# Moving four squares, filling products and three expert layers in the hand-made order of a fused attention and mixture kernel

## The chip, the cores and the metric

One core of a Trainium2 chip runs the whole program. The metric is the device time of one launch in microseconds, the median of several runs. The engines are named as in the profile: PE (TensorE), DVE (VectorE), ACT (ScalarE), POOL (GpSimd), and SP (SyncE), which here issues every DMA.

## The reference

Three stages follow one another. Attention with a block mask over 64 heads, 576 rows of 64; a soft mixture of eight experts over the 4608 resulting rows of 512; then a gated product with three matrices.

```python
scores = np.where(mask, scale * q @ k.T, -1e9)          # mask: blocks of 64
x = softmax(scores) @ v                                  # -> 4608 x 512
logits = x @ phi                                         # 32 slots
slot_input = softmax(logits, 0).T @ x                    # 32 x 512
for e in range(8):                                       # 4 slots each
    slot_out[e] = np.maximum(slot_input[e] @ w1[e], 0) @ w2[e]
x = softmax(logits, 1) @ slot_out
out = ((x @ w1_) * (x @ w2_)) @ w3 @ w_out
```

As only 32 slots exist, the last line is computed by way of products of pairs of slots: w3 and w_out are multiplied once (1024 x 512), and pairs of slots are weighted with it.

## The kernel before, in words

The core handles the 64 heads as 32 pairs, four pairs to a batch. `Plan` holds one entry for every operation: its engine, an estimated duration, what it comes after, and a due time from the tables `OFF`, `EARLY`, `LATE`, `TAIL` and `POST`. `order()` plays this plan through with its own estimates and writes out one list, and each engine executes its part of the list strictly in that order. "After" entries shape only this list; on the chip an instruction waits for the data and buffers that it truly uses. PE has two queues in the plan, `row` (sorted by due time) and `fill` (the products `W`); a `W` is taken whenever it fits ahead of the next row entry.

Names that the change touches, in order of time:

- `M0`-`M3`, `mT`, `Q0`-`Q3`: coarse scores for row maxima, the turning of these maxima, and the exact scores of a pair. `warm` issues products of zeros on PE ahead of such an operation. `run` does so where the plan saw PE idle for over 0.5 us ahead of an `M`, a `Q` or an `mT` of pairs 0 and 1: before `M2` of pair 0 (4 products of 256 columns), `M3` of pair 1 (1), `M1` of pair 1 (2) and `mT` of pair 0 (6).
- `E0`-`E3` (ACT, line 607): exponentials of the scores. `V0`, `V1` (PE, line 632): their products with v, copied out by `c0`, `c1` (ACT, line 641). `lgT` (PE, line 706) turns a batch's logits; `LTe` (ACT, lines 771 to 776) is its exponential.
- `bl`, `bm`, `b1` to `b4`: the background. 28 times, SP loads 512 KB of a 64-bit weight (`bl`, line 1026); ACT squares its high halves (`bm`, line 1039), DVE does three bit operations (`b1` to `b3`), and `b4` combines both. `bm` and `b1` wait for the load.
- `wl` 0 to 15 (SP, line 1058): 2 MB of expert weights each, first layers even, second layers odd, into five windows used in turn; `wl` i waits for the layer that used its window. `rl` (SP, line 1084): twelve pieces of w3 of 512 KB into buffers freed by products `W`, squared by `nq` (ACT, line 1097), rebuilt by `n1` to `n4` (DVE), split by `ph` (ACT) and `pl` (POOL, both by helper lines 1045 and 1047).
- `W` (PE, line 1134): 192 products of w3 with w_out. Piece i is the twelve products 12i to 12i+11. The list takes pieces 0, 2, 4, 6, then 1, 3, 5, 7, then 8 to 15. Three products are kept for the last stage, and five more wait for the last second layer.
- `L1`, `L2` (PE, lines 1155 and 1176): first and second layer of expert e. Between them lie `hs`, `hT`, `re` (ACT, PE, ACT). In the list before, `L1` 2 stands behind `W` 12, `L1` 3 behind `W` 22, and `L1` 4 behind `W` 60.
- `so`, `sS`, `sd`, then four times `ab`, `ac`, `aT`, `aa`, `ad`: the slots' outputs are multiplied with w1_ and w2_ in four sums `ab` (PE, line 1200), copied (`ac`), turned (`aT`, PE, line 1211) and taken apart by ACT (`aa`) and DVE (`ad`, both line 1216). The list has `ab` 0, `aT` 0, `ab` 1, `aT` 1 and so on. `G` 0 on DVE is the first product of slot pairs, and `ad` 1 stands behind it. All four turns write one PSUM bank.
- Then, outside the plan, the sums over pairs (PE, line 1296) and the output's products (line 1359).

Of the kernel before, what the change touches and what calls it, by code (L numbers as in the profile page):

```python
# [27 lines left out]
SP = 640  # L28
# [3 lines left out]
def warm(nc, keep, ps, n, w=128):  # L32

    for _ in range(n):
        nc.tensor.matmul(ps[:, 0:w], lhsT=keep["zeros"][:, 0:128], rhs=keep["zeros"][:, 0:w], start=True, stop=True)
# [5 lines left out]
           M2=(-125.6823, -227.9619, -295.6467, -206.3959), M3=(-194.0205, -267.9342, -226.9977, -208.1606),  # L41
# [9 lines left out]
           M2=(-2844.3708, -1088.7161, -992.9072, -317.549), M3=(-2623.525, -1855.0865, -787.0927, -742.624),  # L51
# [31 lines left out]
WAIT = dict(PE=0.0, DVE=10616.85007, ACT=6722.41331, POOL=7334.5673, SP=12439.66901)  # L83
PERIOD, HELD, SLIP, WIN0, WIN1 = 100.0, 8, 0.1, 20, 29
BG0, BGS = 3.0, 1.0
BESIDE = {8: 0, 9: 2, 26: 4, 27: 6}
LATE_W3 = [i for i in range(16) if i not in BESIDE.values()]
PLACE = (0, 4, 1, 5, 2, 6, 3, 7)
# [11 lines left out]
class Plan:  # L100
# [136 lines left out]
    def experts(self, N):  # L237
        B = N // NP_B - 1
        quarter = lambda x: [f"{x}{i}" for i in range(4)]
        scores = lambda *ns: [(q, n) for n in ns for q in quarter("Q")]  # L240
        pair = lambda n: [(x, n) for x in ("V0", "V1", "SU", "P0", "P1", "P3")]
        at = lambda n, x: [(x, n)] if n >= 0 else []
        op = lambda name, n, *a, **k: self.op((name, n), *a, **k)
        free = {i: pair(N - 2 + PLACE[i] // 3) for i in range(8) if PLACE[i] < 6}
        free[5] = [("ts", 1), ("lt", 2), ("LTe", B - 1), ("lgT", B - 1)]
        free[7] = [("lt", 3), ("la", 3), ("cTd", B - 1)]
        out = {0: [("sub", N - 2)], 1: [("sub", N - 1)], 2: [("V0", N - 3), ("V1", N - 3), ("cT", B - 1)], 3: [("pl", 0), ("pl", 2)],
               **{c: [("mI", 0), ("ws", 0)] for c in range(4, 8)}}
        win = {0: [("Q0", 6)], 1: scores(N - 4, N - 3), 2: scores(N - 2, N - 1), 3: scores(N - 1) + [(f"sx{i}", B - 1) for i in range(4)], 4: [("S", B - 1)] + [(x, n) for n in (N - 2, N - 1) for x in ("V0", "V1")]}
        for i in range(16):  # L250
            self.due = lambda t: (WIN0 if i == 0 else WIN1 if i < 4 else N) * PERIOD + (POST[f"wl{i}"] if i else 0.)
            op("wl", i, "SP", .4, win[i] if i in win else [(("L1", "L2")[(i - 5) % 2], (i - 5) // 2)], lat=2.5, load=4.97)
            if i < 4:
                self.due = lambda t: N * PERIOD + POST["zm"] + i
                op("zm", i, "POOL", .5, win[i] + [("pl", 6)] * (i == 0))
        self.due = lambda t: N * PERIOD + POST[t]
        for c in range(8):
            op("wh", c, "ACT", .55, [("b4", c)] + out[c], due=f"wh{c}")
            op("wo", c, "POOL", 1.26, [("wh", c)], due=f"wh{c}")
        for i in range(16):  # L260
            f, g = divmod(i, 2)
            t = self.due
            if i in LATE_W3:
                q = LATE_W3.index(i)
                prev = LATE_W3[q - 1] if q else None
                op("rl", i, "SP", .43, free[i] if i < 8 else [("W", 24 * (f - 4) + 12 * g + 11)], lat=2.5, load=1.25, due=f"rl{i}")
                op("nq", i, "ACT", .62, [("rl", i)] + [("b4", 27) if q == 0 else ("n4", prev)], due=f"nn{i}")
                op("n1", i, "DVE", .69, [("rl", i), ("n4", prev) if q else ("wr", 0)], 1, due=f"nn{i}")
                op("n2", i, "DVE", .69, [("n1", i)], due=f"nn{i}", late=.1)
                op("n3", i, "DVE", .69, [("n2", i)], due=f"nn{i}", late=.2)  # L270
                op("n4", i, "DVE", .69, [("n3", i), ("nq", i)] + [("pl", LATE_W3[q - 2]) if q > 1 else ("b3", 27)], free="n1", due=f"nn{i}", late=.3)
            op("ph", i, "ACT", .58, [("n4", i)] if i in LATE_W3 else [("b4", next(j for j in BESIDE if BESIDE[j] == i))] + free[i], due=f"ph{i}")
            op("pl", i, "POOL", 1.26, [("ph", i)], due=f"ph{i}")
        order = [(f, j) for g in (0, 12) for f in range(4) for j in range(g, g + 12)] + [(f, j) for f in range(4, 8) for j in range(24)]
        for n, (f, j) in enumerate(order[:-LATER]):
            c, i = divmod(j, 3)
            deps = [("ph", 2 * f + c // 4)] if j % 12 == 0 or f == 0 else []
            if j % 12 == 2:
                deps += [("pl", 2 * f + c // 4)]
            if n >= len(order) - HELD:  # L280
                deps += [("L2", 7)]
            if f == 0:
                deps += [("wh", c)] if i == 0 else [("wo", c)] if i == 1 else []
            op("W", 24 * f + j, "PE", .2325, deps, int(j == 0), filler=True, due="W")
        for f in range(7):
            op("We", f, "ACT", .5, [("W", 24 * f + 23), ("wo", f)], free=("W", 24 * f), due="We", late=10. * f)
            if f > 3:
                op("Wh", f, "ACT", .55, [("We", f)], due="Wh", late=10. * f)
                op("Wl", f, "POOL", 1.26, [("Wh", f)], due="Wh", late=10. * f)
        for e in range(8):  # L290
            op("L1", e, "PE", 1.75, [("wl", 2 * e), ("sC", 0)] + at(e - 1, "L2"), 1, mode="quarters", due="L", late=100. * e)
            op("hs", e, "ACT", .3, [("L1", e)] + at(e - 2, "hT"), free="L1", due="L", late=100. * e + 10)
            op("hT", e, "PE", .2, [("hs", e)], 1, due="L", late=100. * e + 20)
            op("re", e, "ACT", .22, [("hT", e), ("zm", e // 2)], free="hT", due="L", late=100. * e + 30)
            op("L2", e, "PE", 1.74, [("re", e), ("wl", 2 * e + 1)], int(e == 0), mode="quarters", due="L", late=100. * e + 40)
        op("so", 0, "ACT", .55, [("L2", 7), ("z6", 0)], free=("L2", 0), due="gh", late=-1.)
        op("sS", 0, "PE", 0.81, [("so", 0), ("hT", 6)], 1, due="end")
        op("sd", 0, "DVE", .25, [("sS", 0)], free="sS", due="end")
        for t in range(4):
            op("ab", t, "PE", .9, [("sd", 0)], 1, mode="quarters", due="end", late=.1 + .4 * t)  # L300
            op("ac", t, "ACT", .25, [("ab", t)], free=("ab", t), due="We", late=-5. - (3))
            op("aT", t, "PE", .1, [("ac", t)], int(t == 0), due="end", late=.3 + .4 * t)
            op("aa", t, "ACT", .4, [("aT", t)], due="We", late=-5. - (4))
            if t < 2:
                op("ad", t, "DVE", .3, [("aT", t)], due="end", late=.5 if t == 0 else .8 + t)
        op("g0", 0, "POOL", .4, [("L2", 7)], due="end")
        op("ow", 0, "DVE", .3, [("L2", 6)], due="end")
        for f in range(4):
            op("gh", f, "ACT", .55, [("We", f), ("L2", 5 if f < 2 else 7)], due="gh", late=10. * f)
            op("gl", f, "POOL", 1.26, [("gh", f)], due="gh", late=10. * f)  # L310
        op("G", 0, "DVE", 2.05, [("aa", 0), ("ad", 0), ("L2", 6)], due="end", late=.7)
        op("Gc", 0, "ACT", .6, [("G", 0)], due="We", late=-5.5)
# [7 lines left out]
    def order(self):  # L320
# [13 lines left out]
        while len(out) < len(ops):  # L334
# [14 lines left out]
                    if best is None or c[0] < best[0]:  # L349
                        best = c[0], e, c[1]  # L350
            t, e, k = best
            o, slot, idle = ops[k], None, t - free[e]
            del ready[e][k]
            end = t + o["dur"]
            if e == "PE":
# [19 lines left out]
            if o["free"]:  # L375
                for i in held[o["free"]]:
                    bank[i] = done[k]
            out.append((t, len(out), k, slot, idle if e == "PE" and k[1] < 2 else 0.))
            for a in then.get(k, ()):
                waits[a] -= 1  # L380
                if not waits[a]:
                    ready[ops[a]["eng"]][a] = max(done[x] for x in ops[a]["after"])
        return [o[2:] for o in sorted(out)]


class Ring:
# [11 lines left out]
class Attn:  # L398
# [581 lines left out]
        self.constants()  # L980

    def run(self):
        for (name, n), slot, idle in Plan(self.nb).order():
            if idle > .5 and (name[0] in "MQ" or name == "mT") and n < 2:
                warm(self.nc, self.keep, self.bank(slot), int(4.5 * idle - 1), 256)
            f = getattr(self, "op_" + name, None) or getattr(self.rest, "op_" + name, None)
            if f:
                f(n, slot)
            else:
                f = getattr(self, "op_" + name[:-1], None) or getattr(self.rest, "op_" + name[:-1])  # L990
                f(n, slot, int(name[-1]) if name[-1].isdigit() else name[-1])
# [555 lines left out]
```

## Time and profile before

| what | value |
|---|---|
| median of 3 runs | 563.34 us (562.89 to 563.6) |
| the profiled execution | 562.72 us, of which the span of its instructions is 560.7 us |
| PE busy | 544.9 us, 97% of the span |
| DVE, POOL, ACT busy | 394.6, 332.6, 322.2 us |
| mean granted PE clock | 0.997 of full speed |
| DMA | 116.97 MB, mean 209 GB/s |

A busy engine has an instruction in flight; it is not thereby at its peak. The idle time before an instruction is shown in brackets with what ended it. The granted clock is given as a share of 2.4 GHz; its other level is 1.2 GHz. Times from here on are microseconds from the start of the span.

### The profile page before, as it was taken

The page shows a single profiled execution, that of the slowest core. Times are in us where ns is not written, and L with a number is a line of the kernel's source. Part 1 is how long each engine was busy: PE and PEld are TensorE (multiplying, and loading weights), DVE is VectorE, ACT ScalarE, POOL GpSimd, SP SyncE. Part 2 cuts the span into 40 slices and gives each one's busy share as a digit, 9 for nine tenths or more (in the row PEclk, how much of TensorE's full clock was granted, in tenths as well). Part 3 has the DMA queues.
Part 4 walks back from the last instruction along what each step waited for, and adds up shares of the span by engine and source line. Part 5 has one row for each costly group of instructions (what it writes and reads, how often), then busy time and mean ns, then how long its engine had stood idle before and what let it go on. Part 6 is the DMA issues. An engine that isn't in the chain of part 4 may idle for free.

```text
span 560.7 us, 14190 instructions
## 1 busy us (share of the span) xinstructions
PE 544.9 (97%) x5527; PEld 407.3 (73%) x5527; DVE 394.6 (70%) x720; ACT 322.2 (57%) x636; POOL 332.6 (59%) x244
## 2 busy tenths in 40 slices
PE   8899999999999999999999989998999999999997
PEld 4777878787878787877778665455568678888885
DVE  5778877898988988988773469207579486665650
ACT  3856768577677696785857624214443355454451
POOL 5798996997978979979976526103530022313220
PEclk9999999999999999999999999989999999999999
DMA  7245685556558465565557977999822058557622
GB/s 251 97 164 178 200 308 177 173 184 210 161 181 233 143 215 191 156 209 167 155 159 259 388 274 288 425 420 427 357 65 77 1 150 263 191 177 252 207 102 110
DMA packets 39514, 116.97 MB, mean 209 GB/s; under 512 B 5532, under 2 KB 15996, under 8 KB 37384
## 3 DMA queue, kind: packets, MB, share of 16 engines
q1 hardware_dynamic: 39448, 116.08, 60.4%
q8 instruction: 43, 0.70, 0.5%
q14 instruction: 23, 0.19, 0.1%
HBM read 105.75 MB, written 10.45 MB: 207 GB/s over the span
## 4 chain that ended last, share of the span: by engine, by line
PE 81%; DMA 10%; DVE 3%; ACT 2%; POOL 1%; issue 1%; SPq 0%; DVEq 0%; ACTq 0%; POOLq 0%
PE ps L1359 16%; PE ps L584 16%; PE ps L632 15%; PE ps L1134 6%; PE ps L526 5%; DMA win<-in_moe_w 4%; PE ps L648 4%; PE ps L1296 3%; PE ps L754 2%; DMA s<-in_w3T 2%; PE ps L1176 2%; PE ps L1155 2%; PE ps L1361 1%; PE ps L803 1%; PE ps L697 1%; DMA vt<-in_w3T 1%
## 5 line engine op out<-in xcount | busy, mean ns | idle before, releaser
L530 DVE TENSOR_REDUCE tc<-ps 128x10 f32<-128x640 f32 (+2 forms) x128 | 122.3, 987 | 26.4 <-PE ps L526 22.4
L607 ACT ACTIVATE s<-ps 128x1024 f32<-128x1024 f32 (+2 forms) x128 | 102.8, 839 | 33.5 <-PE ps L584 25.9
L584 PE MATMUL ps<-set 64*128 64x320 f32 (+4 forms) x1152 | 103.1, 297 | 0.2 <-ACT s L607 0.2
L513 POOL TENSOR_TENSOR set<-raw,set 128x1152 fp32r<-128x1152 f32 x32 | 85.0, 2660 | 8.9 <-ACT set L506 7.2
L584 PEld LDWEIGHTS ps<-set 64*128 64x128 f32 (+1 forms) x1152 | 83.0, 177 | 5.6 <-ACT s L607 0.5
L617 POOL TENSOR_TENSOR tc<-tc,s 128x384 f32<-128x384 f32 (+1 forms) x63 | 80.7, 1281 | 4.5
L617 POOL TENSOR_TENSOR tc<-s,s 128x640 f32<-128x640 f32 x32 | 50.0, 1562 | 32.1 <-ACT s L607 22.2
L632 PE MATMUL ps<-s,xw 128*64 128x320 f32 (+3 forms) x528 | 64.1, 384 | 1.0 <-ACT s L607 1.0
L1359 PE MATMUL ps<-H,pB 128*128 128x512 f32 x216 | 53.9, 396 | 0.4 <-POOL pB L1339 0.4
L1359 PE MATMUL ps<-H,pA 128*128 128x512 f32 x216 | 53.0, 395 | 0.0
L632 PEld LDWEIGHTS ps<-s,xw 128*64 128x64 f32 x528 | 34.4, 137 | 24.0 <-ACT s L607 1.4
L584 PE MATMUL ps<-shift 64*128 64x320 f32 (+3 forms) x320 | 51.5, 318 | 0.0
L526 PE MATMUL ps<-set 64*128 64x320 f32 (+5 forms) x384 | 47.9, 326 | 1.7 <-ACT set L506 1.3
L1372 ACT COPY s<-ps 128x512 f32<-128x512 f32 x35 | 20.5, 587 | 49.0 <-PE ps L1361 48.9
L1359 PEld LDWEIGHTS ps<-H,pB 128*128 128x128 f32 x216 | 40.5, 188 | 11.0 <-POOL pB L1339 1.1
L1359 PEld LDWEIGHTS ps<-H,pA 128*128 128x128 f32 x216 | 40.6, 188 | 9.9 <-DVE pA L1339 0.3
L1339 POOL TENSOR_TENSOR pB<-wx,pB 128x384 fp32r<-128x384 f32 x12 | 15.3, 1279 | 50.9 <-ACT pB L1334 50.9
L526 PEld LDWEIGHTS ps<-set 64*128 64x128 f32 (+1 forms) x384 | 32.0, 188 | 7.9 <-ACT set L506 2.0
L506 ACT CAST set<-raw 128x1152 fp32r<-128x1152 f32 x31 | 35.8, 1155 | 2.1 <-DMA raw<-in_qk 2.1
L1107 DVE TENSOR_SCALAR ps<-s 128x512 int32<-128x512 int32 x12 | 8.4, 699 | 32.9 <-DMA s<-in_w3T 32.6
L584 PEld LDWEIGHTS ps<-shift 64*128 64x128 f32 x320 | 30.7, 187 | 0.7 <-ACT xw L641 0.2
L1339 POOL TENSOR_TENSOR pA<-xw,pA 128x384 fp32r<-128x384 f32 x10 | 12.4, 1236 | 30.7 <-ACT pA L1334 30.7
(282 smaller groups left out, 1059.3 us busy)
## 6 DMA issues: line engine op xcount, KB each, us to landing
win<-in_moe_w SPq DMA_DIRECT2D x13, 2048.0 KB
raw<-in_qk SPq DMA_DIRECT2D x32, 576.0 KB
vt<-in_moe_w SPq DMA_DIRECT2D x16, 512.0 KB
out<-s SPq DMA_DIRECT2D x16, 512.0 KB
shift<-rr SPq DMA_DIRECT2D x56, 144.0 KB
xw<-in_v SPq DMA_DIRECT2D x22, 320.0 KB
xw<-in_moe_w SPq DMA_DIRECT2D x3, 2048.0 KB
s<-in_w3T SPq DMA_DIRECT2D x12, 512.0 KB
```

Source lines behind the costliest of these rows:

```text
L506: self.nc.scalar.copy(hi, self.raw[n])
L513: self.nc.gpsimd.tensor_tensor(lo, self.raw.pop(n), hi.bitcast(F32), op=ALU.subtract)
L526: self.nc.tensor.matmul(ps[0:m, h, o:o + kn], lhsT=qh[r, q0:q0 + m], rhs=kh[r, k0:k0 + kn], start=True, stop=True)
L530: self.nc.vector.tensor_reduce(self.bmb[n % 2][:, :, o:o + m // 64], self.st.pop(("M", n, i))[:, :, 0:m].rearrange("p h (n k) -> p h n k", ...
L584: mm = lambda h, o, n, lt, rt, m=128, **k: self.nc.tensor.matmul(ps[0:m, h, o:o + n], lhsT=lt, rhs=rt, **k)
L607: self.nc.scalar.activation(out=out, in_=ps[:, :, 0:sum(g[3] for g in self.UNITS[u])], func=AF.Exp, scale=SCALE)
L617: eng.tensor_tensor(acc[:, :, lo:hi], a, b, op=ALU.add)
L632: mm(ps[64 * h:64 * h + 64, q0 - lo:q1 - lo], lhsT=v[:, 128 * j + 64 * h:128 * j + 64 * h + 64], rhs=pt[:, h, o:o + q1 - q0], start=j == 0 ...
L648: mm = lambda g, o, rhs, **k: self.nc.tensor.matmul(ps[32 * g:32 * g + 32, o:o + rhs.shape[-1]], lhsT=one, rhs=rhs, **k)
L1134: self.nc.tensor.matmul(self.st["W", f], lhsT=a[:, o], rhs=b, start=j == 0, stop=j == 23)
L1339: eng.tensor_tensor(Pl[:, k], raw(u)[1][:, k], Ph[:, k].bitcast(F32), op=ALU.subtract)
L1359: nc.tensor.matmul(ps, lhsT=a[:, k, r], rhs=b[:, k], start=k + i == 0, stop=False)
```

## The change

- A table `SQUARED` moves `bm` of four background loads a step later in ACT's order, behind a named entry: load 3 behind `c1` of pair 5, load 11 behind `LTe` of batch 2, load 16 behind `E1` of pair 20, load 27 behind `E1` of pair 31. What follows from `bm` and stood ahead of the new place (`b1`, `b2`) moves with it.
- A table `FILL` replaces the rule for the products of zeros: 6, 9, 4 and 10 of them ahead of the four operations named above, and 9 ahead of `M2` of pair 2, each of 192 columns instead of 256.
- `BEHIND` lets the first layers of experts 2, 3 and 4 come after `W` 23, 47 and 71, the ends of pieces 1, 3 and 5. `FIRST` adds 1.5 us to the plan's estimate for the load `wl` 5.
- The turns `aT` are due 0.3 us later, behind the next sum: `ab` 0, `ab` 1, `aT` 0, `ab` 2, `aT` 1, `ab` 3, `aT` 2, `aT` 3.

```diff
+SQUARED = {3: ('c1', 5), 11: ('LTe', 2), 16: ('E1', 20), 27: ('E1', 31)}
+FIRST, BEHIND = 1.5, {('L1', 2): 23, ('L1', 3): 47, ('L1', 4): 71}
+FILL = {("M2", 0): 6, ("M3", 1): 9, ("M1", 1): 4, ("mT", 0): 10, ("M2", 2): 9}
...
-            op("wl", i, "SP", .4, win[i] if i in win else [(("L1", "L2")[(i - 5) % 2], (i - 5) // 2)], lat=2.5, load=4.97)
+            op("wl", i, "SP", .4, win[i] if i in win else [(("L1", "L2")[(i - 5) % 2], (i - 5) // 2)], lat=2.5, load=4.97 + FIRST * (i == 5))
...
+        behind = lambda x, e: [("W", BEHIND[x, e])] if (x, e) in BEHIND else []
-            op("L1", e, "PE", 1.75, [("wl", 2 * e), ("sC", 0)] + at(e - 1, "L2"), 1, mode="quarters", due="L", late=100. * e)
+            op("L1", e, "PE", 1.75, [("wl", 2 * e), ("sC", 0)] + at(e - 1, "L2") + behind("L1", e), 1, mode="quarters", due="L", late=100. * e)
...
-            op("aT", t, "PE", .1, [("ac", t)], int(t == 0), due="end", late=.3 + .4 * t)
+            op("aT", t, "PE", .1, [("ac", t)], int(t == 0), due="end", late=.6 + .4 * t)
...
+        for j, k in SQUARED.items():
+            where = {o[0]: i for i, o in enumerate(out)}
+            i, to = where["bm", j], where[k]
+            assert i < to
+            after = [out[i]] + [out[n] for n in sorted(where[a] for a in ops if ("bm", j) in ops[a]["after"] or ("b1", j) in ops[a]["after"]) if n < to]
...
+            out[to + 1:to + 1] = after
+            for x in after:
+                out.remove(x)
...
-            if idle > .5 and (name[0] in "MQ" or name == "mT") and n < 2:
-                warm(self.nc, self.keep, self.bank(slot), int(4.5 * idle - 1), 256)
+            if (name, n) in FILL:
+                warm(self.nc, self.keep, self.bank(slot), FILL[name, n], 192)
```

## Rows read from the trace of the kernel before

**Rows 1.** The page, busy time, share of the span and instructions of each engine.

```profile
PE 544.9 (97%) x5527; PEld 407.3 (73%) x5527; DVE 394.6 (70%) x720; ACT 322.2 (57%) x636; POOL 332.6 (59%) x244
```

**Rows 2.** The windows: length, five engines' busy time (instructions), clock, DMA share, GB/s.

```profile
100.00:200.00 100.00, 98.90 (x1382) 78.02 (x1378) 87.39 (x162) 71.24 (x141) 89.67 (x60) 1.00 0.59 183
...
300.00:350.00 50.00, 47.31 (x467) 32.18 (x467) 32.16 (x77) 25.17 (x59) 25.52 (x23) 1.00 0.81 312
350.00:380.00 30.00, 27.94 (x228) 15.21 (x220) 3.46 (x5) 6.30 (x16) 2.57 (x2) 0.94 1.01 425
```

**Rows 3.** The timeline of PE, start: start, length, instruction, idle before and releaser.

```profile
11.30 1.91 PE L546 MATMUL ps<-ident,wx 128*1 128x128 f32 x8
...
15.59 0.67 PE L526 MATMUL ps<-set 64*128 64x320 f32 x6 [1.34 <-ACT set L506]
...
16.20 1.03 PE L546 MATMUL ps<-ident,wx 128*1 128x128 f32 x8
```

**Rows 4.** The timeline of ACT around the squares of loads 3 and 16.

```profile
73.90 1.03 ACT L607 ACTIVATE s<-ps 128x1024 f32<-128x1024 f32 x1 [0.93 <-POOL tc L617]
...
203.24 0.68 ACT L1039 ACTIVATE vt<-vt 128x512 bf16<-128x512 f32 x1 [0.56 <-DVE tc L536]
```

**Rows 5.** The timeline around the square of load 11.

```profile
157.32 0.69 ACT L1039 ACTIVATE vt<-vt 128x512 bf16<-128x512 f32 x1 [1.59 <-DMA vt<-in_moe_w]
...
159.14 0.68 ACT L641 COPY wx<-ps 128x320 f32<-128x320 f32 x2
...
159.87 0.33 PE L706 MATMUL ps<-ident,s 128*128 128x128 f32 x1 [0.88 <-ACT wx L641]
```

**Rows 6.** The timeline from the square of load 27 to the last maxima.

```profile
305.65 0.27 PE L584 MATMUL ps<-shift 64*128 64x192 f32 x2
...
307.13 0.71 ACT L1039 ACTIVATE vt<-vt 128x512 bf16<-128x512 f32 x1 [1.45 <-DMA vt<-in_w3T]
...
307.73 1.63 ACT L607 ACTIVATE s<-ps 128x1024 f32<-128x1024 f32 x2
...
309.40 2.16 PE L632 MATMUL ps<-s,xw 128*64 128x320 f32 x16 [1.05 <-ACT s L607]
...
329.17 0.66 ACT L1097 ACTIVATE vt<-s 128x512 bf16<-128x512 f32 x1 [6.60 <-DMA s<-in_w3T]
...
330.06 0.27 PE L886 MATMUL ps<-ident,wx 64*128 64x64 f32 x1 [1.65 <-ACT wx L881]
```

**Rows 7.** The windows of the DMA: stretch, length, clock, DMA share, GB/s.

```profile
318.00:320.00 2.00, 1.00 0.99 279
```

**Rows 8.** The chain that ended last, experts to sums: start, length, what.

```profile
361.71 24.84 DMA win<-in_moe_w
...
404.64 1.92 PE ps L1176 x16
...
416.08 1.01 PE ps L1200 x32
...
417.87 3.24 PE ps L1134 x14
421.11 1.82 PE ps L1296 x8
```

**Rows 9.** The timeline of PE and ACT in the experts' stage and the turns.

```profile
365.30 3.36 PE L1155 MATMUL ps<-win,siT 128*32 128x256 f32 x32 [2.06 <-DMA win<-in_moe_w]
...
385.56 0.73 PE L1134 MATMUL ps<-wx,s 128*128 128x512 f32 x2 [1.40 <-ACT s L1047]
...
387.88 0.69 ACT L1097 ACTIVATE vt<-s 128x512 bf16<-128x512 f32 x1 [1.81 <-DMA s<-in_w3T]
...
405.78 0.70 ACT L1097 ACTIVATE vt<-s 128x512 bf16<-128x512 f32 x1 [2.34 <-DMA s<-in_w3T]
...
415.78 0.30 PE L1211 MATMUL ps<-ident,tc 128*128 128x128 f32 x1 [0.83 <-DVE tc L1216]
```

**Rows 10.** The windows after the wait at 365.30, columns as in rows 2.

```profile
366.00:369.00 3.00, 3.00 (x29) 1.33 (x22) 0.00 (x0) 0.25 (x1) 0.00 (x0) 0.50 1.02 431
```

More of the change, by code (lines that the diff above doesn't have):

```diff
@@ L294, in experts @@
             op("re", e, "ACT", .22, [("hT", e), ("zm", e // 2)], free="hT", due="L", late=100. * e + 30)
-            op("L2", e, "PE", 1.74, [("re", e), ("wl", 2 * e + 1)], int(e == 0), mode="quarters", due="L", late=100. * e + 40)
+            op("L2", e, "PE", 1.74, [("re", e), ("wl", 2 * e + 1)] + behind("L2", e), int(e == 0), mode="quarters", due="L", late=100. * e + 40)
         op("so", 0, "ACT", .55, [("L2", 7), ("z6", 0)], free=("L2", 0), due="gh", late=-1.)
@@ L351, in order @@
             t, e, k = best
-            o, slot, idle = ops[k], None, t - free[e]
+            o, slot = ops[k], None
             del ready[e][k]
@@ L377, in order @@
                     bank[i] = done[k]
-            out.append((t, len(out), k, slot, idle if e == "PE" and k[1] < 2 else 0.))
+            out.append((t, len(out), k, slot))
             for a in then.get(k, ()):
@@ L382, in order @@
                     ready[ops[a]["eng"]][a] = max(done[x] for x in ops[a]["after"])
-        return [o[2:] for o in sorted(out)]
+        out = [o[2:] for o in sorted(out)]
+        for j, k in SQUARED.items():
[3 more added lines that the diff above has]
+            after = [out[i]] + [out[n] for n in sorted(where[a] for a in ops if ("bm", j) in ops[a]["after"] or ("b1", j) in ops[a]["after"]) if n < to]
+            assert not any(x[0] in ops[y[0]]["after"] for x in after for y in out[:to + 1] if y not in after)
+            out[to + 1:to + 1] = after
+            for x in after:
+                out.remove(x)
+        return out
 class Ring:
@@ L982, in run @@
     def run(self):
-        for (name, n), slot, idle in Plan(self.nb).order():
-            if idle > .5 and (name[0] in "MQ" or name == "mT") and n < 2:
-                warm(self.nc, self.keep, self.bank(slot), int(4.5 * idle - 1), 256)
+        for (name, n), slot in Plan(self.nb).order():
+            if (name, n) in FILL:
+                warm(self.nc, self.keep, self.bank(slot), FILL[name, n], 192)
             f = getattr(self, "op_" + name, None) or getattr(self.rest, "op_" + name, None)
```

## The prediction

> **What bounds the kernel.** I read the page first: PE has an instruction in flight for 97% of the span [rows 1], so only its idle time and the time in which it runs slowly can be won. The windows show where these lie: 1.1 us between 100 and 200, 2.7 between 300 and 350, 2.1 between 350 and 380, where the granted clock is also below one and the DMA is full at 425 GB/s [rows 2]. The timeline of each place names the waits: one behind the square of load 11 [rows 5], one behind that of load 27 and one after it [rows 6], one for an expert's weights and one for a piece of w3 [rows 9]. The chain of what ended last runs through the experts' loads: one is issued at 361.71 and lands 24.84 later [rows 8]. From there on the DMA queue sets the layers, and PE fills up with products `W`.
>
> The last second layer (`L2` of expert 7) starts at 404.64 [rows 8]. The last piece of w3, queued right behind its weights, has landed by 405.78, and a piece takes about 1.3 us: one lands by 387.88, after the load that lands at 386.55 (361.71 + 24.84) [rows 8, 9]. So these weights landed near 404.5, and PE reaches the layer just as they come. Two things must therefore move: the load stream, and the PE work left behind it.
>
> **The filling products.** The eight transposes of pair 0 take 1.91 us at 11.30, those of pair 1 take 1.03 at 16.20 [rows 3]: PE still works at the lower level, 1.2 GHz, at 11.30 and at the higher by 15.59. 192 columns are 0.16 us at the lower level and 0.08 at the higher. At the lower level, the additions cost 128, 1472, 256 and 384 columns, 1.87 us, and the nine ahead of `M2` of pair 2 take 1.44 where PE idles 1.34 [rows 3]; with nothing else covered, +2.0. If PE comes to the higher level before the transposes, they gain 0.88 (1.91 - 1.03), and ten products of 192 columns take 0.80 there instead of six of 256 at 1.28: -1.4. PE leaves the lower level between two places in this trace after work with short gaps, and the additions close these gaps, so I take -0.4.
>
> On this the Trainium skill ("TensorE: Matmul & The Clock Gate", "Part 1") says that the throttled clock is the default and that activity releases it. By that rule the denser filling brings the whole 1.4, and the sum below would give 558.1; by the row at 11.30, still slow after 10 us of products, the whole 2.0 could be lost, which would give 561.5.
>
> **The squares.** Load 11: ACT waits 1.59 us for it, squares, does the exponentials of `LTe` (157.90 to 159.14, 1.24 us), then two copies; PE waits 0.88 for these [rows 5]. Behind the change `LTe` goes first. If its input is there when ACT becomes free (155.73), the copies start 1.24 earlier and all 0.88 are won; if only at 157.32, nothing. I take 0.6, as the maxima on DVE take part of that wait.
>
> Load 27: ACT waits 1.45 us; the scores for `E1` are ready at 305.92 (305.65 + 0.27) [rows 6]. `E1` can run ahead of the load's landing at 307.13; the square and `E2` then follow, and the products at 309.40 start near 308.6: 0.8 won (0 to 1.05). What follows is a load: ACT waits 6.60 for the first late piece, and PE 1.65 for a copy behind it on ACT [rows 6]. That piece is behind a window load which is issued when the products free its buffer. Between 318 and 320 the DMA moved 279 GB/s where 425 is full [rows 2, 7], a hole of 2 x (1 - 279/425) = 0.69 us; an earlier issue fills it, so 0.65 of the 0.8 passes on (0 if the hole is not the buffer's).
>
> Load 3: its square gets behind a copy that needs a product still running, so it starts later. ACT idles 0.93 before 73.90 for POOL [rows 4], which covers the 0.69 of a square; without that cover the exponential there would be 0.7 late. Load 16: ACT's 0.56 goes [rows 4], but PE does not wait behind it: 0. The DVE steps that move keep their order among DVE's own, and so does the issue of the next background load.
>
> Up to the first expert that is -0.4 - 0.6 - 0.65 = -1.65, as PE is dense between and the start of the load stream moves with it.
>
> **The experts' layers.** Eleven, thirteen and eleven products come ahead of `L1` 2, 3 and 4. A product is 0.231 us (3.24/14) [rows 8]. Queued behind these layers on SP are their windows' next loads; they are issued 2.5 to 3 us later, but a load waits 24.84 in the queue [rows 8], so the stream does not run dry. With that, 11 products (2.5 us) cover the wait of 2.06 before `L1` 4. Behind that wait PE worked 3.00 us at a granted clock of 0.50, the lower level [rows 10], half of it lost: 1.5, which goes too. Piece 9 comes earlier, since the product that frees its buffer is `W` 23, so the wait of 1.40 at 385.56 [rows 9] goes. Together that is 5.0 us, 21 products.
>
> The same order has a price. Pieces 9, 11, 13 and, I expect, 15 are now issued ahead of loads they stood behind. Each takes 1.25 us from the loads that follow, but only the last piece newly passes the last load: `L2` 7 gets +1.25 - 1.65 = -0.4, at 404.2.
>
> PE meanwhile has these 5.0 us, and 1.25 between the two shifts, for products: 159 stand before `L2` 7 in the old list, so 159 + 27 could be done by then; the plan holds back five of its 189 until `L2` 7, so about 184 are. Then hardly any is left behind it.
>
> **Sums ahead of turns.** Turn 2 waits at 415.78 for a copy on DVE [rows 9] that stands behind the first product of slot pairs. This wait stays, whatever is put ahead of it. Behind it in the old list stand a sum (1.01), two products, a turn and 14 products (3.24), until the sums over pairs start at 421.11 [rows 8]. In the new list the sum has run before, and the products too. From turn 2's end (416.08) the last turn remains, 0.3 to 0.6 with its copy: 416.6 instead of 421.1, hence -4.4 against the same `L2` 7. The first turn comes after one sum more, but five products fewer: level, between -0.4 and +0.5. The slot products on DVE begin no later; PE is behind them now, by more than this.
>
> Sum: -0.4 - 4.4 = -4.8; I give back 0.6 for waits that a reordered queue leaves: -4.2. The profiled execution took 562.72, its span 560.7 and 2.0 around it; it goes to 558.5. It lies 0.62 below the median, from which I forecast 563.34 - 4.2 = 559.1, with 557.6 to 560.6 for this case: by their bounds the filling can take 1.0 more off or add 2.4, and the squares 0.7 or 1.25, but hardly all on one side.
>
> **Rivals.**
> - *The clock falls at the turns.* With the products gone, PE has nothing to do between the last sum and turn 2: the 0.83 of before [rows 9], six absent products (1.4), less the sum put ahead (1.0), so 1.2 us. For it: a wait of 2.06 was followed by a granted clock of 0.50 [rows 9, 10]. Against: this one is shorter, and five products remain for it. Price 1.5: 560.6. Chance 0.10.
> - *The products do not move.* The list is made with estimates; if it places as many before `L2` 7 as before, PE waits at the layers, and only the early gains and the 0.83 at turn 2 [rows 9] remain: 1.2 with piece 15 ahead, 2.5 without, so 560.8 to 562.1, at 561.5 in the middle. For it: the DMA is full either way [rows 2]. Chance 0.18.
> - *A square stops the layers: slower.* If the square of piece 9, now earlier in ACT's list, stands ahead of the copies of `L1` 3, ACT waits there for a piece that lands only after the weights of `L1` 4 (365.30 + 1.25 - 1.65 = 364.9), and PE waits with it from about 360: 5 us, then 1.5 of clock, with no product to cover it. That turns -4.2 into +2.3: 565.6. It decides from a wait of some 3 us on. For it: the same happened at 329.17, 6.60 on ACT and 1.65 on PE [rows 6]. Against: by my count of the plan's estimates the piece is ready some 4 us after those copies, so ACT gets its square behind them. Chance 0.10.
>
> **Numbers.** The forecast's case has 0.62. What a measurement of this kernel can tell from no change is about 0.2%, 1.1 us. Faster by more: 0.62, 0.10 and 0.12 of the second rival, 0.84; within: 0.06 of it and 0.01 of the third, 0.07; slower: 0.09. The range 557.5 to 561.9 holds the first case, the first rival and two thirds of the second.
>
> **What would show it.** Transposes of pair 0 near 1.0 us (filling); no wait of ACT for background loads 11 and 27 ahead of their exponentials, PE's waits at 159.87 and 309.40 shrunk; `L1` 4 without a wait and at a granted clock of 1.00; `L2` 7 near 404, with PE waiting for weights before it; under ten products between `L2` 7 and the sums over pairs, which start near 416.5. It is wrong if PE again waits over 1 us at one layer, if `L2` 7 comes later than 405, or if many products still lie behind it.

## The result and the profile after

The changed kernel takes 554.95 us (median of 4 executions, 554.24 to 555.33), the kernel before beside it 563.12 (561.35 to 563.6); the ratio is 0.9859, 95% interval 0.9835 to 0.9883. The forecast was 559.1 with a range from 557.5: the direction is right, the gain is 8.2 us instead of 4.2. The profiled executions differ by 7.4 (562.72 and 555.33), their spans by 7.3.

The page of the changed kernel, busy times [rows 1]; below it the windows [rows 2], columns as there.

```profile
PE 542.7 (98%) x5552; PEld 407.1 (74%) x5552; DVE 392.4 (71%) x720; ACT 322.3 (58%) x636; POOL 332.6 (60%) x244
```

```profile
300.00:350.00 50.00, 49.35 (x462) 33.91 (x463) 34.07 (x80) 26.06 (x62) 25.52 (x23) 1.00 0.85 330
350.00:380.00 30.00, 30.00 (x248) 16.53 (x247) 11.22 (x17) 9.67 (x22) 5.16 (x4) 1.00 1.01 424
```

PE now idles 0.65 us where it idled 2.69, and nowhere between 350 and 380, at full granted clock. Two starts of the kernel before that are compared below, the exact scores of pair 0 and the sums over pairs:

```profile
17.47 0.50 PE L584 MATMUL ps<-shift 64*128 64x512 f32 x2
...
420.95 1.98 PE L1296 MATMUL ps<-g_stage 128*128 128x512 f32 x8
```

The timeline of the changed kernel, start to turns (lines moved by 14: L584 is L598 and so on):

```profile
10.88 1.03 PE L560 MATMUL ps<-ident,wx 128*1 128x128 f32 x8 [0.15 <-DVE wx L552]
...
14.20 0.67 PE L540 MATMUL ps<-set 64*128 64x320 f32 x6 [0.77 <-ACT set L520]
15.36 1.03 PE L560 MATMUL ps<-ident,wx 128*1 128x128 f32 x8 [0.49 <-DVE wx L552]
...
16.64 0.50 PE L598 MATMUL ps<-shift 64*128 64x512 f32 x2
...
146.56 0.69 ACT L1053 ACTIVATE vt<-vt 128x512 bf16<-128x512 f32 x1 [2.20 <-DMA vt<-in_moe_w]
147.40 1.16 ACT L520 CAST set<-raw 128x1152 fp32r<-128x1152 f32 x1
148.61 0.42 PE L540 MATMUL ps<-set 64*128 64x320 f32 x2 [1.04 <-ACT set L520]
...
159.55 0.33 PE L720 MATMUL ps<-ident,s 128*128 128x128 f32 x1
...
328.19 0.27 PE L900 MATMUL ps<-ident,wx 64*128 64x64 f32 x1 [0.65 <-ACT wx L895]
...
336.32 1.93 PE L1169 MATMUL ps<-win,siT 128*32 128x256 f32 x32
...
364.78 1.93 PE L1169 MATMUL ps<-win,siT 128*32 128x256 f32 x32
...
403.60 1.92 PE L1190 MATMUL ps<-win,win 128*32 128x512 f32 x16
...
409.61 0.33 PE L1225 MATMUL ps<-ident,tc 128*128 128x128 f32 x1
...
412.14 0.33 PE L1225 MATMUL ps<-ident,tc 128*128 128x128 f32 x1
412.89 0.33 PE L1225 MATMUL ps<-ident,tc 128*128 128x128 f32 x1 [0.42 <-ACT tc L1230]
413.50 2.11 PE L1310 MATMUL ps<-g_stage 128*128 128x512 f32 x8 [0.28 <-ACT g_stage L1290]
```

The exact scores start 0.83 us earlier (17.47 before), but a late background load takes that back at 148.61, and at 159.55 only 0.32 is left [rows 5]. At 300 nothing is left: the same products of a later pair's scores start at 299.68 in the kernel before and at 299.93 in the changed one, 0.25 behind:

```profile
299.68 0.70 PE L584 MATMUL ps<-set 64*128 64x320 f32 x6
...
299.93 0.70 PE L598 MATMUL ps<-set 64*128 64x320 f32 x6
```

The waits of [rows 6] shrink (1.05 to none, 1.65 to 0.65), and the experts start at 336.32 instead of 338.20. `L1` 4 and the products after it do not wait [rows 9]; `L2` 7 starts at 403.60 instead of 404.64 [rows 8], the sums over pairs at 413.50 instead of 420.95. That lead stays: the last output products follow the sums at the same distance as before, within 0.15.

Marks of all traces that the text uses, read from their timelines: turn of batch 0's logits, first `L1`, `L2` 7, sums over pairs, and the distance between the last two.

| kernel | logits 0 | `L1` 0 | `L2` 7 | sums | `L2` 7 to sums |
|---|---|---|---|---|---|
| before | 83.05 | 338.20 | 404.64 | 420.95 | 16.3 |
| changed | 82.23 | 336.32 | 403.60 | 413.50 | 9.9 |
| b_fill | 82.29 | 335.89 | 402.61 | 418.93 | 16.3 |
| b_sq | 86.95 | 340.71 | 409.94 | 426.27 | 16.3 |
| b_layers | 86.82 | 341.05 | 410.11 | 421.12 | 11.0 |
| b_at | 84.86 | 338.95 | 405.56 | 420.43 | 14.9 |
| a_noat | 82.73 | 336.76 | 404.70 | 415.71 | 11.0 |
| a_ad1 | 82.18 | 335.47 | 403.54 | 413.43 | 9.9 |
| a_pool | 82.02 | 335.12 | 402.68 | 413.11 | 10.4 |
| a_l4 | 81.92 | 334.12 | 401.70 | 411.60 | 9.9 |

### The profile page after: what moved, and what is told of

It is laid out like the page before. It is cut to its first block, busy times and chain, and to the rows that moved or that the text cites. A ratio compares the mean times of both kernels' runs of the same rounds, so it can differ in the third digit from the quotient of the medians.

```text
span 553.4 us, 14238 instructions
## 1 busy us (share of the span) xinstructions
PE 542.7 (98%) x5552; PEld 407.1 (74%) x5552; DVE 392.4 (71%) x720; ACT 322.3 (58%) x636; POOL 332.6 (60%) x244
## 4 chain that ended last, share of the span: by engine, by line
PE 83%; DVE 8%; DMA 4%; ACT 2%; issue 2%; POOL 0%; SPq 0%; DVEq 0%; ACTq 0%; POOLq 0%
PE ps L598 17%; PE ps L1373 16%; PE ps L646 15%; PE ps L1148 8%; PE ps L540 5%; PE ps L662 4%; PE ps L768 3%; PE ps L1190 3%; PE ps L1169 3%; DVE tc L544 2%; DMA s<-in_w3T 2%; PE ps L711 2%; PE ps L1375 1%; PE ps L817 1%; DMA vt<-in_moe_w 1%
## 5 line engine op out<-in xcount | busy, mean ns | idle before, releaser
L598 PE MATMUL ps<-set 64*128 64x320 f32 (+4 forms) x1152 | 103.3, 297 | 0.2 <-ACT s L621 0.2
L598 PEld LDWEIGHTS ps<-set 64*128 64x128 f32 (+1 forms) x1152 | 83.1, 177 | 5.6 <-ACT s L621 0.5
L598 PE MATMUL ps<-shift 64*128 64x320 f32 (+3 forms) x320 | 51.6, 319 | 0.0
L540 PE MATMUL ps<-set 64*128 64x320 f32 (+5 forms) x384 | 46.6, 319 | 2.1 <-ACT set L520 1.8
L1059 POOL TENSOR_TENSOR s<-vt,s 128x512 fp32r<-128x512 f32 x12 | 15.6, 1299 | 29.3 <-ACT s L1061 15.4
L598 PEld LDWEIGHTS ps<-shift 64*128 64x128 f32 x320 | 30.7, 187 | 0.7 <-ACT xw L655 0.2
```

The lines of the kernel that those rows point to most:

```text
L540: self.nc.tensor.matmul(ps[0:m, h, o:o + kn], lhsT=qh[r, q0:q0 + m], rhs=kh[r, k0:k0 + kn], start=True, stop=True)
L598: mm = lambda h, o, n, lt, rt, m=128, **k: self.nc.tensor.matmul(ps[0:m, h, o:o + n], lhsT=lt, rhs=rt, **k)
```

## The experiments

Names with b_ are the kernel before with a part of the change, those with a_ the changed kernel with something else. A ratio and the two bounds of its 95% interval stand in brackets; ratios, and the gains given as minus so many us, are against executions of the kernel before on the same chip; over all experiments these are 91, with medians from 563.1 to 564.7 by chip and 563.7 in all. The changed kernel's median over its 15 executions, from three groups on different chips, is 555.02.

**Each part alone.**

b_layers, only these (and what uses them):
```diff
+FIRST, BEHIND = 1.5, {('L1', 2): 23, ('L1', 3): 47, ('L1', 4): 71}
```


> The kernel before with only the experts' layers changed (first layers 2 to 4 behind pieces 1, 3 and 5, and the larger estimate for load 5). Theory A, PE's ledger: what is won is PE's idle and half-speed time, and a product that is only moved is worth nothing. Here the waits of 2.06 and 1.40 and the 1.5 lost to the clock go (5.0), but the second half of the turns still waits for a copy on DVE behind the first slot product, now without products to cover it: some 3.1 us of idle between the last second layer and the sums over pairs instead of 0.83; net -2.7, sums over pairs 12 us behind the last second layer. Theory B, the products: what counts is that 25 of them no longer lie behind the last second layer, and the turns do not matter: sums over pairs 10 us behind it, net -5.5.

Measured: 559.84 (ratio 0.9934, 0.9907 to 0.9961), -3.3, in time nearer to theory A. The distance of 11.0 lies midway between the theories, and the four turns wait 1.74 in all where theory A had 3.1:

```profile
415.74 0.33 PE L1225 MATMUL ps<-ident,tc 128*128 128x128 f32 x1 [0.43 <-ACT tc L1217]
417.46 0.33 PE L1225 MATMUL ps<-ident,tc 128*128 128x128 f32 x1 [0.39 <-ACT tc L1217]
419.34 0.30 PE L1225 MATMUL ps<-ident,tc 128*128 128x128 f32 x1 [0.53 <-DVE tc L1230]
421.04 0.33 PE L1225 MATMUL ps<-ident,tc 128*128 128x128 f32 x1 [0.39 <-ACT tc L1217]
```

b_at:
```diff
-late=.3 + .4 * t)
+late=.6 + .4 * t)
```


> The kernel before with only the turns one sum later. In its list the copy of turn 1 on DVE now stands behind turn 2, in the list before it stood ahead of it. Theory A: turn 2's wait of 0.83 goes and nothing else, as the products behind the last second layer are still there: -0.8. Theory B: the wait belongs to the slot product and shows up one step later: 0 (within 0.2 us).

Measured: 562.31 (0.9981, 0.9949 to 1.0013), which alone says nothing; in the trace the distance falls by 1.4.

b_sq:
```diff
+SQUARED = {3: ('c1', 5), 11: ('LTe', 2), 16: ('E1', 20), 27: ('E1', 31)}
```


> The kernel before with only the four squares moved. Theory A: the waits of 0.88 at the logits of batch 2, 1.05 at the last products with v and about 1.0 of the 1.65 at the last maxima go, some of it is lost in between; first expert 1.9 us earlier and the end as much: -1.9. Rival, the loads pace the experts: the lead at the first expert is eaten by waits for weights before the last second layer: 0.

Measured: 562.17 (0.9982, 0.9951 to 1.0013), -1.0, between the two and not told from none.

b_fill:
```diff
+FILL = {("M2", 0): 6, ("M3", 1): 9, ("M1", 1): 4, ("mT", 0): 10, ("M2", 2): 9}
```


> The kernel before with only the products of zeros changed. Theory A: the first exact scores come 0.8 us earlier, and the lead lasts only until a background load is late for its square (in the changed kernel the square of load 10 waited 2.2 us for its transfer at 146.6, and the lead of 0.8 became a lag of 0.4): -0.2 to +0.4 at the end. Rival: that late transfer is of one execution or belongs to the moved squares, and the 0.8 lasts: -0.8.

Measured: 560.07 (0.9948, 0.9925 to 0.9971), -3.1: more than either theory. The windows of the first 26 us say why. First b_fill, then b_at and b_sq, which have the old start:

```profile
8.00:16.00 8.00, 6.21 (x59) 4.26 (x58) 7.63 (x17) 3.68 (x7) 4.42 (x3) 1.00 0.68 243
16.00:22.00 6.00, 6.00 (x82) 5.28 (x82) 5.02 (x8) 4.65 (x8) 3.53 (x2) 1.00 0.53 183
```

```profile
8.00:16.00 8.00, 4.99 (x39) 3.00 (x38) 7.64 (x17) 3.62 (x7) 4.36 (x2) 0.97 0.70 247
16.00:22.00 6.00, 6.00 (x49) 5.10 (x46) 2.71 (x6) 3.44 (x7) 3.35 (x2) 0.50 0.59 191
```

```profile
8.00:16.00 8.00, 6.39 (x32) 3.60 (x30) 6.78 (x16) 3.90 (x7) 3.35 (x2) 0.50 0.65 237
16.00:22.00 6.00, 6.00 (x42) 4.30 (x42) 3.65 (x6) 2.07 (x5) 4.40 (x2) 0.50 0.39 118
```

With the old start the granted clock is 0.50 from 16 to 22 behind a wait of 1.90 at 14.11 (b_at), or from 8 on behind short waits (b_sq), and the logits of batch 0 come 2.6 and 4.7 us behind b_fill's. The profiled execution of the kernel before was another kind: low from the start, up by 15.59, without a second fall [rows 3], and only 0.8 behind. Its mean clock was 0.997, which the 1.5 us lost at [rows 10] alone make of 560.7: a low start does not show in this mean. Of the 91 executions of the kernel before, 14 had 0.996 or more (median 562.3), 44 had 0.990 to 0.995 (563.1), 33 less (565.3). All 15 of the changed kernel had 0.999 or 1.000.

These groups explain only a part of the 3.1. On the chip of b_fill, 7 executions of the kernel before with 0.996 or more have a median of 562.53, 14 with 0.990 to 0.995 one of 562.50, 14 with less 565.29, and 563.13 is the median of all; b_fill's twelve, all at 0.996 or more, have 560.07. So the falls that the mean clock shows are worth some 0.6, and the low start 0.8 in the traces. The rest, some 1.7, stays open; in the two profiled executions b_fill's experts begin 2.3 earlier, and there 0.88 is the wait for load 11, which b_fill's trace does not have, and 0.6 a shorter wait at the last maxima (1.05 for 1.65). Whether the filling brings that about is not shown.

**The start.** f_m2 and f_rest split the filling:

```diff
f_m2:   the old rule, and ("M2", 2): 9
f_rest: FILL without ("M2", 2)
```


> The kernel before with only one place of the new filling: nine products of zeros of 192 columns ahead of M2 of pair 2, where PE waits 1.3 to 1.9 us; the other places as before. The filling alone took 3.1 us off the median, and the traces of kernels with the old start show granted clocks of 0.50 for about 7 us behind that wait in two executions and from 8 us on, behind three short waits, in a third. Theory C, one wait: the clock falls behind the wait ahead of M2 of pair 2, so this place alone brings nearly all: -2.5 to -3, mean clock of all executions at 0.996 or more. Theory D, all waits of the first 16 us: the short ones ahead of it bring the clock down too in a part of the executions, and this place brings a part: about -1.5, with clocks from 0.987 up.

> The kernel before with the new filling at all its places but the one ahead of M2 of pair 2. Theory D, all waits of the first 16 us matter: PE is at the higher level from about 5.5 us on and falls behind the open wait of 1.5 to 1.9 us at 14, in most executions: -0.5 to -1.5, clocks about 0.991. Theory C, that one wait decides: no better than before, -0.3 to +0.3. If neither holds and the denser start alone keeps the clock up: -3, clocks at 0.996 or more.

Measured: f_m2 561.19 (0.9967, 0.9946 to 0.9988), -1.9; f_rest 562.50 (0.9976, 0.9944 to 1.0007), -1.3. That is as theory D has it, each brings a part, though f_rest's alone is not told from none; executions of both still show clocks from 0.990. In f_m2's trace the clock is 0.58 and 0.56 from 8 to 12, behind the short waits, and it is full at 12 and stays so behind the filled place.

a_nofill and a_nofill_again are the changed kernel with the old rule.

> The changed kernel with the old products of zeros. Theory E, the parts add: the filling is worth 3.1 as alone, 558.0, clocks spread as in the kernel before. Rival: what the start wins is lost at late background loads, as in the two profiled executions, where the lead of 0.8 was gone by 154 us: 555 to 555.4.

> The changed kernel with the old products of zeros, once more. If the filling is worth as much within the change as alone: +2.5 to +3.5 against the changed kernel. If the smaller figure holds: +0.8 to +1.8. In either case executions with clocks under 0.996 are the slower ones and those above stand 0.5 to 1 behind the changed kernel.

> The changed kernel itself, beside the three others of this group: 554.9, ratio 0.985 to 0.986.

Measured: 556.22 (0.9877, 0.9847 to 0.9907) and 558.89 (0.9887, 0.9859 to 0.9916), the changed kernel beside the second one 555.44 (0.9841, 0.9814 to 0.9867). Over both, 12 executions have a median of 557.35, +2.3 against 555.02, with clocks from 0.990 to 1.0. Against the changed kernel the first group is 1.2 slower (on another chip) and the second 3.4 (on the same); their ratios to the kernel before hardly differ. The filling's worth inside the change lies somewhere between; these runs can't tell where.

**The rest undone.** a_noat and a_nolayers take back the edits of b_at and b_layers, a_nosq that of b_sq, a_nofirst sets FIRST to 0.

> The changed kernel with the turns where they were, so that the copy of turn 1 stands ahead of turn 2 on DVE again, while no products are left there. Theory A, PE's ledger: turn 2 waits for this copy behind the first slot product, and the short waits of the turns for their copies are uncovered: sums over pairs 11.5 to 12 us behind the last second layer instead of 9.9, +1.6 to +2.1, 556.6 to 557.1. Theory B, what counts is only that the products are gone: +0.4 at most, 555.0 to 555.4.

> The changed kernel without the new order of the first layers and without the larger estimate. Theory E, the parts add: the order is worth 3.3 as alone, 558.3. Theory A, PE's ledger: alone it still paid some 1.7 at the turns, which the later turns take away, so here its absence costs the whole 5.0 of waits and slow clock: 559.5 to 560.

> The changed kernel with the four squares back in their old places. If the parts add: +1.0, 555.9, with waits for loads 11 and 27 ahead of their exponentials and 1.0 to 1.5 us of PE at the last products with v. Rival: load 27 is late for its new place too in many executions, and the layers take up the rest: within 0.3 of the changed kernel.

> The changed kernel itself, beside the three others of this group. Theory F: the wait for background load 10 in its profile (2.20 us on ACT, 1.04 on PE behind it) is of that execution; here another load is late (14 or 18, as in two other kernels) or none. PE idles 0.2 to 1.5 us between 140 and 305; time 554 to 556, the granted clock of every run at 0.996 or more.

> The changed kernel without the larger estimate for load 5: piece 15 of w3 goes behind load 14 instead of ahead of it, 180 products instead of 184 stand ahead of the last second layer. If a piece ahead of a load costs 1.25 as the prediction charged: the last second layer comes up to 1.25 earlier, less the four products that now lie behind it (0.9), -0.3. If PE's ledger is all that counts: the products only move, 0 to +0.5 for waits that four products no longer cover.

Measured against 555.02: a_noat 555.99 (0.9871, 0.9842 to 0.9901), +1.0, between the theories, with the distance at 11.0; a_nolayers 557.59 (0.9899, 0.9868 to 0.9930), +2.6, nearer to the parts adding (3.3), and theory A's 5 is not seen; a_nosq 556.18 (0.9880, 0.9842 to 0.9919), +1.2, though two of its six executions, the slowest, had a mean clock of 0.993 with the new filling in place; a_nofirst 556.55 (0.9867, 0.9837 to 0.9897), +1.5, of which its trace explains 0.4 (the distance is 10.3 instead of 9.9); after_again 554.91 (0.9853, 0.9818 to 0.9889), with load 10 late by 1.39 on ACT and nothing of it on PE.

**The turns.** a_ad1 restores only the wait that the prediction kept; a_pool puts POOL beside the first slot product:

```diff
a_ad1:
-op("aT", t, "PE", .1, [("ac", t)],
+op("aT", t, "PE", .1, [("ac", t)] + [("ad", 1)] * (t == 2),
a_pool, in op_G:
+if f == 0:
+    tcw = self.attn.tcw
+    self.nc.gpsimd.tensor_tensor(self.Gr(3)[0], tcw[:, 1024:1536], tcw[:, 1024:1536], op=ALU.subtract)
```


> The changed kernel with turn 2 (and turn 3) listed behind the copy of turn 1 on DVE, the sums still ahead of the turns. Theory A, this order alone makes the wait that the prediction kept: turn 2 waits for the copy, some 2.4 us behind the first turn's, and the sums over pairs come 10.7 to 11.2 us behind the last second layer instead of 9.9: +0.8 to +1.3. Rival, the order of the sums against the turns brings the gain: 9.9 to 10.1, +0 to +0.2.

> The changed kernel with one more subtraction on POOL (128x512, its result is overwritten), which starts when the first turn's copy on DVE is done and runs beside the first slot product. Theory G: a slot product with both inputs in SBUF waits until POOL's operation is over; one of the three steps takes 1.6 to 1.8 us instead of 0.69, the sums over pairs come 10.8 to 11.1 us behind the last second layer instead of 9.9, and the time is +0.9 to +1.1 against the changed kernel (554.9). Rival: the two engines run beside each other, 9.9 and no change; the 1.79 of the kernel before was something else.

Measured: a_ad1 554.59 (0.9820, 0.9794 to 0.9846), no slower than the changed kernel. Theory A fell: the wait is back, the distance is 9.9 all the same.

```profile
413.14 0.41 PE L1225 MATMUL ps<-ident,tc 128*128 128x128 f32 x2 [0.99 <-DVE tc L1230]
```

a_pool 555.26 (0.9835, 0.9803 to 0.9867): not told from the changed kernel in time, but its trace shows the mechanism at half the size expected, a distance of 10.4. First the kernel before, where POOL splits the last piece of w3, then a_pool, then b_at, where the split falls beside a later slot product, and last the changed kernel, where no POOL instruction runs beside it:

```profile
412.25 0.69 DVE L1266 TENSOR_TENSOR g_stage<-tc 128x512 f32<-128x512 f32 x1 [0.45 <-ACT tc L1216]
412.86 1.79 DVE L1267 TENSOR_TENSOR g_stage<-tc 128x512 f32<-128x512 f32 x1
...
412.81 1.29 POOL L1045 TENSOR_TENSOR s<-wO,s 128x512 fp32r<-128x512 f32 x1 [1.19 <-ACT s L1047]
```

```profile
409.49 1.04 POOL L1288 TENSOR_TENSOR g_stage<-tc 128x512 fp32r<-128x512 f32 x1 [1.04 <-DVE tc L1230]
...
409.86 1.22 DVE L1280 TENSOR_TENSOR g_stage<-tc 128x512 f32<-128x512 f32 x1 [0.45 <-ACT tc L1230]
411.00 0.68 DVE L1281 TENSOR_TENSOR g_stage<-tc 128x512 f32<-128x512 f32 x1
```

```profile
417.93 1.42 POOL L1059 TENSOR_TENSOR s<-wO,s 128x512 fp32r<-128x512 f32 x1 [5.37 <-ACT s L1061]
418.11 1.78 DVE L1283 TENSOR_TENSOR g_stage<-g_stage 128x512 f32<-128x512 f32 x1
```

```profile
410.77 0.69 DVE L1280 TENSOR_TENSOR g_stage<-tc 128x512 f32<-128x512 f32 x1 [0.45 <-ACT tc L1230]
411.38 0.69 DVE L1281 TENSOR_TENSOR g_stage<-tc 128x512 f32<-128x512 f32 x1
```

POOL ends at 414.10, 410.53 and 419.35, DVE's product at 414.65, 411.08 and 419.89: 0.54 to 0.55 later each time, whatever the overlap. The Trainium skill ("SBUF — State Buffer", "Who interferes with whom") says that a DVE instruction with two inputs in SBUF contends with a GpSimd instruction that reads SBUF, and that the ports that they share are an exclusive lock; the traces agree.

**Further.** sq_more moves five more squares; a_l4 moves the square of the first late piece of w3 behind the small copy of the last logits (`l4`):

```diff
sq_more:
+SQUARED: 6: ('c1', 9), 10: ('c1', 13), 14: ('c1', 17), 18: ('c1', 21), 22: ('c1', 25)
a_l4, at the end of order():
+where = {o[0]: i for i, o in enumerate(out)}
+i, to = where["nq", 1], where["l4", 0]
+out.insert(to, out.pop(i))
```


> The changed kernel with the squares of loads 6, 10, 14, 18 and 22 also a step later, behind two copies and the cast of the next pair's input. Theory F: each of these loads is late in some executions by up to 2.4 us, and PE then waits about 1.1 for the cast behind the square; with the squares behind the cast that goes, and the median gains 0.3 to 1.0 against the changed kernel. Rival: the square's own followers become the next ones late (the copy of the queries behind it, the next load's issue): no gain, -0.2 to +0.5.

> The changed kernel with the square of the first late piece of w3 behind the small copy of the last logits on ACT instead of ahead of it. If the wait of 0.65 to 1.5 us at the last maxima (in all traces of the changed kernel and of its variants with both tables but one) is all that stands there: -0.6 to -1.2, 553.7 to 554.3. Rival: the weights of the later experts' layers then end the waits, or the next copies become late: 0, within 0.3.

Measured: sq_more 555.37 (0.9851, 0.9817 to 0.9886), no gain, as the rival says; in its trace PE waits 1.18 elsewhere, behind a copy. a_l4 554.04 (0.9818, 0.9783 to 0.9852): 1.0 under the changed kernel's 555.02, as the first expectation has it (the changed kernel did not run on this chip; a_pool did, with 555.26). Its six executions lie between 553.48 and 554.66, those of the changed kernel between 554.24 and 557.57. The wait is gone, and the experts begin 1.6 to 2.2 earlier than in the changed kernel's three traces (334.12 against 335.75 to 336.32):

```profile
325.76 0.27 PE L903 MATMUL ps<-ident,last_L 128*128 128x128 f32 x1
325.97 0.27 PE L904 MATMUL ps<-ident,wx 64*128 64x64 f32 x1
```

## Why the prediction was wrong

**The step that failed most by the two traces: "hence -4.4 against the same `L2` 7".** The distance fell by 6.4, from 16.3 to 9.9. The prediction made it 11.9, because it carried the time of turn 2 over from the kernel before as a fixed one ("This wait stays"): 11.14 behind `L2` 7 (415.78 less 404.64). In the changed kernel turn 2 comes 8.54 behind `L2` 7 and waits for nothing, as it now stands ahead of that copy on DVE. But that is not what the 2.0 hang on, for the distance is 9.9 with the wait restored, too. There (a_ad1) turn 2 comes at 9.60, 1.54 earlier than carried over. Of this, 1.05 lies between the first turn and turn 2: it is the slot product ahead of the copy, which takes 1.79 us beside POOL's split of the last piece of w3 in the kernel before, and 0.68 without it. That split belongs to the products, and when these go ahead of `L2` 7 it goes too. The other 0.5 is the first turn, 6.0 instead of 6.5 behind `L2` 7, which the prediction took as level. Another 0.5 lies behind turn 2: the sums start 0.3 after it (413.43 for 413.14) instead of 0.8. The prediction moved the products and forgot what ran for them on other engines. The order of the sums brought its part too: with the old turns all four wait, three of them for their own copy on ACT (a_noat, 11.0).

**The second: "so I take -0.4" for the filling.** The working was right for the execution it was read from (0.83 at the exact scores, within the bounds; the 1.4 by the Trainium skill's "TensorE: Matmul & The Clock Gate", "Part 1", was off by a little more, 0.6 against 0.4, but nearer to what the median gained). The profiled execution of the changed kernel did not keep the 0.83 up to the experts (0.25 behind at 300). But the execution that the working was read from showed one kind of start of several. The filling also takes away the starts in which the clock comes up and falls again, and is worth 3.1 us of the median alone and some 2.3 within the change; what of this is not the clock stays open (b_fill). The four parts alone add up to 3.3 + 0.8 + 1.0 + 3.1 = 8.2, as much as the whole, but two of them are not told from none, so the agreement is a rough one. As the profiled execution of before lies near the median all the same (why is not shown), these two misses are not to be added.

**By the traces** the difference of 3.2 between 558.5 and 555.33 is 2.0 for the turns, 0.6 for `L2` 7 (403.60 for 404.2), and the 0.6 given back, which was not needed; the rest is rounding. Of the 0.6 at `L2` 7, 0.2 were won up to the first expert (1.88 for 1.65) and 0.4 behind it, where the layers cost 0.84 instead of 1.25.

**Layers: right in mechanism.** The three waits and the slow stretch vanished as forecast. `L2` 7 is set otherwise than said: PE does not wait for its weights. From `L1` 0 to `L2` 7 the distance grew from 66.4 to 67.3, which is PE's own work: 25 products more (5.8 at 0.231) less the 5.0 of waits and slow clock. In this pair of traces the price of 1.25 for piece 15 is not seen, and a_nofirst gives no gain for taking it away.

**Squares: the sum near by luck, the places not.** Up to the first expert the prediction had 1.65 and the traces show 1.88. But of the 1.0 that filling and load 11 were to bring, nothing was left at 300 (-0.25), and behind it 2.1 were won at the two waits of [rows 6], where the prediction let 0.65 pass on. That 0.65 was the hole in the DMA between 318 and 320, read from its rate alone. The row's DMA share is 0.99 [rows 7], so its engines were not idle there; and in the changed kernel the same stretch moves 336 GB/s, so the hole was not filled either. Load 27 keeps ACT waiting 0.95 to 1.92 in all seven traces with the old place, 0.57 at most with the new one. Load 11 does so in two of seven; in other traces it is another, such as 6, 10, 14 or 18. The 0.6 for load 11 was read from one execution's bad luck.

**Rivals.** The clock did not fall at the turns (0.70 us of waits in all), the products moved (five are left behind `L2` 7, as counted), and no square stopped the layers.

## What to carry to other kernels

Where one engine is busy 97% of the time, keep a ledger of its idle and half-speed time. Here are three windows of the kernel before, then of the changed one:

```profile
305.00:340.00 35.00, 32.31 (x308) 22.76 (x304) 21.38 (x58) 15.90 (x41) 17.77 (x18) 1.00 0.75 284
340.00:404.00 64.00, 60.24 (x480) 33.78 (x477) 29.70 (x46) 22.45 (x49) 20.87 (x17) 0.97 0.99 414
404.00:420.00 16.00, 15.13 (x185) 9.85 (x184) 10.82 (x21) 7.52 (x22) 5.46 (x6) 1.00 0.24 74
```

```profile
305.00:340.00 35.00, 34.35 (x317) 24.35 (x317) 23.07 (x62) 17.68 (x45) 19.90 (x20) 1.00 0.81 303
340.00:404.00 64.00, 64.00 (x499) 36.25 (x501) 30.66 (x46) 23.73 (x49) 21.52 (x17) 1.00 0.98 409
404.00:420.00 16.00, 15.31 (x190) 11.26 (x183) 9.38 (x22) 5.78 (x19) 2.94 (x4) 1.00 0.32 95
```

In them 2.0, 3.8 and 0.2 us of idle vanished, and 1.5 of slow clock, 7.5 together. From 300 on the changed kernel gained 7.7: it was 0.25 behind there, and its sums over pairs came 7.45 earlier. A moved product is worth only the gap that it fills. When work is moved, move its helpers on the other engines in the estimate too, with the contention that they cause. Before costing a repair at the start of a kernel, or at one late load, look at the mean clocks of all runs and at more than one trace: the profiled execution shows one outcome of several.

## What the runs showed of the hardware

In the profile of before, the granted clock reads 1.00 from the start, while the twelve products at 5.35 take 1.91 us and the same twelve 1.10 in b_at: ahead of the first recorded change only durations tell the level. A wait of 1.90 us (b_at), and a row of waits of 0.2 to 0.5 (b_sq), were each followed by a granted clock of 0.50 for over 5 us. Neither always is: b_at has such a row too, from 5.19 to 10.52, without a fall behind it, and a wait of 1.62 in f_rest was followed by the full clock and eight transposes in 1.03. The lines are of before, of b_at (two) and of f_rest:

```profile
5.35 1.91 PE L526 MATMUL ps<-set 64*128 64x320 f32 x12 [0.36 <-ACT set L509]
...
5.19 1.10 PE L540 MATMUL ps<-set 64*128 64x320 f32 x12 [0.21 <-ACT set L523]
...
14.11 0.67 PE L540 MATMUL ps<-set 64*128 64x320 f32 x6 [1.90 <-ACT set L520]
...
15.11 0.67 PE L540 MATMUL ps<-set 64*128 64x320 f32 x6 [1.62 <-ACT set L520]
```

Why the old start goes one way or another from execution to execution, and why other background loads are late each time, stays open.
